# A fused attention and maxout kernel: sums of exponentials tested on chip, with a branch to a recomputing part

## The chip, the cores and the metric

The kernel runs on one core of one Trainium2 chip. The metric is the device time of one launch in microseconds (us); where several runs are shown, their median. The core has five engines with their own instruction streams: TensorE (PE in the profile; PEld are its weight loads), VectorE (DVE), ScalarE (ACT), GpSimd (POOL) and SyncE (SP). SP and POOL issue the DMA transfers here. Engines wait for one another through semaphores.

## The reference

`x` has shape (8, 8, 512, 64) and `state` (8, 8, 32, 64): batch B, head H, rows, depth D. Attention runs in both directions, then a feed-forward part takes the maximum of three products:

```python
scores = scale * np.matmul(x, state.transpose(0, 1, 3, 2))
scores = scores - scores.max(-1, keepdims=True)
a = np.exp(scores)
a /= a.sum(-1, keepdims=True) + 1e-09
xread = np.matmul(a, state)
scores2 = scale * np.matmul(state, x.transpose(0, 1, 3, 2))
# the same softmax over scores2 gives a2
sread = np.matmul(a2, x)
attn = np.concatenate([xread, sread], axis=2)
# heads side by side: 8 * 544 tokens of 512 values
h = np.maximum(np.maximum(x @ w1, x @ w2), x @ w3)
out = h @ w_out
```

The weights `w1`, `w2`, `w3` are 512 x 768 and `w_out` is 768 x 512. The output is 4352 x 512 in float32. The entries of `x` and `state` are normal draws times 0.1.

## The kernel before, in words

The kernel does not subtract the maximum. It takes exp(scale * score) directly (`scores`, L176), sums over the 32 states (`softmax`, L183, tile `den`), and divides. For the other direction (`sread`, L207) it uses the same exponentials as weights, with a block of ones behind `x` that gives the sum over the 512 rows in the same product; its reciprocal is `rd` (L221).

The attention read and the first feed-forward product are joined: `g_cols` forms G = state times the three weight matrices (tile `G`), and `x_maxout` (L270) multiplies G by the transposed attention weights `aT`, which gives the three products for 512 tokens and 128 of the 768 hidden columns at once. Each call of `maxout` (L253) has three accumulators in PSUM (`pw0`, `pw1`, `pw2`). ACT copies the first to SBUF (L264), DVE takes the maximum with the second (L267) and then with the third (L268), into `ht`. `s_maxout` does the same for the 256 state tokens of all batches. `ffn_out` multiplies `ht` by `w_out` (L285), ACT copies the result to `osb` (L292), and a DMA writes it out (L301, L296). The last piece is shared: ACT copies one half (L289) and DVE the other (L290).

PSUM tiles with the tag `pw` rotate through four buffers; the three accumulators of `maxout`, the output accumulator `po` and several transposes all take from these four.

The order of work on each engine is the order in which the Python code records it (the schedule is manual); each engine takes its instructions strictly in that order. The main loop (L382 on) goes over batches 2 to 7. In each it calls `x_maxout(b, m)` for m = 0 to 5, and after each m the functions that were put in `slots[m]`. For the last batch, b = 7, the slots hold `s_maxout(m)` and, for m = 1, 2, 4 and 5, `ffn_out` of the batch before. So around m = 1 of the last batch, PE's queue holds: six matmuls of `x_maxout(7, 1)`, twelve of `s_maxout(1)`, six of `ffn_out(6, 0)`, then six of `x_maxout(7, 2)`. After the loop come six calls of `ffn_out`, and then the end of the program: SP waits for the semaphores of all engines and DMA queues one after another, and two barriers over all engines follow.

Of the kernel before, what the change touches and what calls it, by code (L numbers as in the profile page):

```python
# [8 lines left out]
F32 = mybir.dt.float32  # L9
BF16 = mybir.dt.bfloat16  # L10
AX = mybir.AxisListType
AF = mybir.ActivationFunctionType


@with_exitstack
def kernel(
# [14 lines left out]
    nc = tc.nc  # L31

    B, H, S, D = x.shape
    _, _, Ns, _ = state.shape
# [7 lines left out]
    J = 4  # L42
    HS = H // 2
    NM = d_ff // 128
    XW = H * J * D
    scale = 1.0 / (D ** 0.5)

    const = ctx.enter_context(tc.tile_pool(name="const", bufs=1))
    data = ctx.enter_context(tc.tile_pool(name="data", bufs=1))
    wpool = ctx.enter_context(tc.tile_pool(name="weights", bufs=1))  # L50
    work = ctx.enter_context(tc.tile_pool(name="work", bufs=2))
    pp = ctx.enter_context(tc.tile_pool(name="pp", bufs=2, space=bass.MemoryType.PSUM))
# [15 lines left out]
    def load_x(b):  # L68
        nc.gpsimd.dma_start(  # L69
            out=x_sb[b][:, 0:XW].rearrange("p (h jd) -> p h jd", h=H),  # L70
            in_=x[b].rearrange("h (p j) d -> p h (j d)", j=J))
# [9 lines left out]
    ident = const.tile([128, 128], BF16, name="ident")  # L81
# [27 lines left out]
    warm = const.tile([128, 1], F32, name="warm")  # L109
    nc.scalar.activation(out=warm, in_=zero[:, 0:1], func=AF.Exp, scale=1.0)  # L110
    ats = data.tile([128, B, HS, Ns], BF16, name="ats")

    def keep_busy(n):
        p = pp.tile([128, 1024], F32, tag="two", name="idle")
        for _ in range(n):
            nc.tensor.matmul(p[:, 0:512], zero[:, 0:128], zero, start=True, stop=True)
# [21 lines left out]
    xT, e, a, aT, G, ht, osb = {}, {}, {}, {}, {}, {}, {}  # L138

    def new(d, b, shape, name, bufs=2):  # L140
        d[b] = work.tile(shape, BF16, tag=name, bufs=bufs, name=name)

    def x_transpose(b, g, copy):

        if g == 0:
            new(xT, b, [128, H, 2, 128], "xT")
        p = pp.tile([128, HS, 2, 128], BF16, tag="pw", bufs=4, name="pxt")
        for s in range(HS):
            for jj in range(2):
                nc.tensor.transpose(  # L150
                    p[:, s, jj, :],
                    xv[b][:, 2 * s + g, 2 * jj:2 * jj + 2, :].rearrange("p j d -> p (j d)"), ident)
        copy(out=xT[b].rearrange("p (s g) j t -> p g s j t", g=2)[:, g], in_=p)  # L153

    def x_transpose_dma(b):
        new(xT, b, [128, H, 2, 128], "xT")
        nc.sync.dma_start_transpose(out=xT[b].rearrange("p h j t -> p (h j) t"), in_=x_sb[b][:, 0:XW])

    def scores(b, g0, g1):
# [7 lines left out]
        for jj in range(2):  # L167
            for g in range(g0, g1):
                for s in range(HS):
# [5 lines left out]
                        stop=(g == g1 - 1 and s == HS - 1), skip_group_check=True)  # L175
        nc.scalar.activation(out=e[b][:, :, g0:g1], in_=p, func=AF.Exp, scale=scale)  # L176

    def softmax(b, g0, g1, mul):
        n = g1 - g0
        if g0 == 0:  # L180
            new(a, b, [128, J, 2, HS, Ns], "a")
        den = work.tile([128, J, n, HS], F32, tag=f"den{n}", name="den")
        nc.vector.reduce_sum(out=den, in_=e[b][:, :, g0:g1], axis=AX.X)  # L183
        rden = work.tile([128, J, n, HS], F32, tag=f"rden{n}", name="rden")
        nc.vector.reciprocal(out=rden, in_=den)  # L185
        mul(  # L186
            out=a[b][:, :, g0:g1].rearrange("p j g s n -> p j (g s) n"),
            in0=e[b][:, :, g0:g1].rearrange("p j g s n -> p j (g s) n"),
            in1=rden.rearrange("p j g s -> p j (g s)").unsqueeze(3).to_broadcast((128, J, n * HS, Ns)))
# [14 lines left out]

    late = []

    def sread(b):  # L207

        p = pp.tile([128, 2, 2, D], F32, tag="pw", bufs=4, name="psr")
        for j in range(J):  # L210
            for g in range(2):
                for s in range(HS):
                    xj = xv[b][:, 2 * s + g, j, :]
                    both = bass.AP(xj.tensor, xj.offset,
                                   (xj.ap[0], (XW - ((2 * s + g) * J + j) * D, 2), (1, D)))
                    nc.tensor.matmul(  # L216
                        p[32 * s:32 * s + 32, g], e[b][:, j, g, s, :], both,
                        start=(j == 0 and g == 0), stop=(j == J - 1), skip_group_check=True,
                        tile_position=(0, 32 * s))
        rd = work.tile([128, 2, 1], F32, tag="rd", name="rd")  # L220
        nc.vector.reciprocal(out=rd, in_=p[:, :, 1, 0:1])  # L221
        sr = work.tile([128, 2, D], BF16, tag="sr", bufs=B, name="sr")
        nc.vector.tensor_mul(out=sr, in0=p[:, :, 0, :], in1=rd.to_broadcast((128, 2, D)))
        late.append(lambda: nc.sync.dma_start_transpose(
            out=ats[:, b].rearrange("p s n -> p (s n)"), in_=sr.rearrange("p g d -> p (g d)")))
# [54 lines left out]
    def ffn_out(b, j, split=False):  # L280
        if j == 0:
            osb[b] = work.tile([128, J, d_model], F32, tag="osb", name="osb")
        p = pp.tile([128, d_model], F32, tag="pw", bufs=4, name="po")
        for m in range(NM):
            nc.tensor.matmul(p, ht[b][:, m, j * 128:(j + 1) * 128], wout_sb[:, m, :],  # L285
                             start=(m == 0), stop=(m == NM - 1))
        o = osb[b]
        if split:
            nc.scalar.copy(out=o[:, j, 0:256], in_=p[:, 0:256])  # L289
            nc.vector.tensor_copy(out=o[:, j, 256:512], in_=p[:, 256:512])  # L290
        else:
            nc.scalar.copy(out=o[:, j, :], in_=p)  # L292
        if b == "s":
            for k in range(4 * j, 4 * j + 4):
                r0 = k * SP + S
                (nc.sync if k % 4 < 2 else nc.gpsimd).dma_start(  # L296
                    out=out[r0:r0 + Ns, :], in_=o[32 * (k % 4):32 * (k % 4) + 32, j, :])
            return
        j0 = j if b == B - 1 and j >= 2 else j - 1
        if j == 1 or j == 3 or j0 == j:  # L300
            (nc.sync if b == B - 1 else nc.gpsimd).dma_start(  # L301
                out=out[b * SP:b * SP + S, :].rearrange("(p j) f -> p j f", j=J)[:, j0:j + 1, :],
                in_=o[:, j0:j + 1, :])


    def late_transposes():
        while late:
            late.pop(0)()

    dve, act, pool = nc.vector.tensor_copy, nc.scalar.copy, nc.gpsimd.tensor_copy  # L310
# [3 lines left out]
    states(0, act)  # L314
    for k in range(1, B // 2):
        nc.vector.memset(bds[k], 0.0)
    keep_busy(4)
    dve(out=x0_sb[0], in_=x0_f)
    x_transpose(0, 0, dve)
# [62 lines left out]
    for b in range(2, B):  # L382
        n = b + 1
        slots = [[] for _ in range(NM)]
        if n < B:
            if n == 3:
                slots[0].append(lambda: x_transpose(n, 0, act))
                slots[0].append(lambda: x_transpose(n, 1, dve))
                slots[3].append(lambda: x_transpose_dma(n + 1))
            elif n + 1 < B:  # L390
                slots[0].append(lambda: x_transpose_dma(n + 1))
            at = 1 if n == 3 else 0
            slots[at].append(lambda: scores(n, 0, 2))
            slots[at].append(lambda: softmax(n, 0, 2, nc.gpsimd.tensor_mul))
            slots[2 if n == 3 else 1].append(lambda: g_cols(n, (0, 1)))
            slots[2].append(lambda: a_transpose_dma(n))
            slots[3].append(lambda: sread(n))
            slots[4].append(lambda: g_cols(n, (2, 3)))
            slots[5].append(lambda: g_cols(n, (4, 5)))
            slots[4].append(late_transposes)  # L400
            if n % 2 and n + 1 < B:
                slots[3].append(lambda: states((n + 1) // 2, act))
            for k in ((4, 5) if n == 3 else (n + 2,)):
                if k < B:
                    slots[0].append(lambda k=k: load_x(k))
        else:
            for m in range(NM):
                slots[m].append(lambda m=m: s_maxout(m))
        for m in (1, 2, 3, 4, 5) if len(pending) > 4 else (1, 2, 4, 5):
            if pending:  # L410
                slots[m].append(lambda t=pending.pop(0): ffn_out(*t))
        for m in range(NM):
            x_maxout(b, m)
            for f in slots[m]:
                f()
        pending += [(b, j) for j in range(J)]
# [4 lines left out]
    ffn_out("s", 1)  # L421
    ffn_out(B - 1, 2)
    ffn_out(B - 1, 3, split=True)


# [28 lines left out]
```

## Time and profile before

| what | value |
|---|---|
| time, median of 3 runs | 166.25 us (166.08 to 167.53) |
| span of the profiled execution, first to last instruction | 164.5 us |
| left between that span and the median | about 1.8 us |
| PE busy | 149.7 us, 91% of the span |
| DVE busy | 96.0 us, 58% |
| ACT busy | 99.1 us, 60% |
| POOL busy | 44.0 us, 27% |

The profiled execution has no time of its own apart from its span; the median minus the span is what the launch adds around it. Busy PE includes the modelled ends of matmuls that overlap, so it is not a share of the peak. An engine's busy time leaves out register, branch, semaphore and DMA-issuing instructions.

### The profile page before, as it was taken

To read this page: it belongs to the slowest core of one execution; us is meant where nothing else is said; L and a number is where in the kernel's file an instruction comes from. 1 tells how busy PE (TensorE), PEld (TensorE's weight loads), DVE (VectorE), ACT (ScalarE), POOL (GpSimd) and SP (SyncE) were. 2 spreads that over 40 slices of the span, in tenths; PEclk is the share of its full clock that TensorE was granted. 3 is DMA by queue.
4 is the path that set the end of the run, shared out by engine and by line. 5 is a ranking of instruction groups with operands and counts; after the bars stand their busy time and mean duration, and the time that the engine had idled before them with its cause. 6 is when DMAs were issued, how large, how long until landed. Compare 5 with 4: busy or idle time off the path is not lost.

```text
span 164.5 us, 3569 instructions
## 1 busy us (share of the span) xinstructions
PE 149.7 (91%) x1432; PEld 70.9 (43%) x1449; DVE 96.0 (58%) x162; ACT 99.1 (60%) x158; POOL 44.0 (27%) x64
## 2 busy tenths in 40 slices
PE   7658699988999999999999999999999999999990
PEld 2425243533445444434344434444444466665430
DVE  4675777889418553665548464865586455585001
ACT  3355578366896678853876688648755853333440
POOL 8975550106150601081016101410141010100140
PEclk9999999999999999999999999999999999999999
DMA  4999999800039999269992989460306030030373
GB/s 132 195 174 199 204 200 248 122 7 0 0 120 130 144 256 198 53 116 145 277 193 87 133 187 104 162 191 14 128 0 195 8 130 0 0 132 0 128 235 148
DMA packets 31824, 20.94 MB, mean 127 GB/s; under 512 B 17184, under 2 KB 29344, under 8 KB 31808
## 3 DMA queue, kind: packets, MB, share of 16 engines
q0 software_dynamic: 15632, 15.08, 46.3%
q1 hardware_dynamic: 16176, 5.64, 18.5%
q8 instruction: 11, 0.18, 0.5%
q14 instruction: 5, 0.04, 0.1%
HBM read 15.20 MB, written 8.91 MB: 147 GB/s over the span
## 4 chain that ended last, share of the span: by engine, by line
PE 63%; DVE 11%; ACT 10%; DMA 6%; POOL 4%; issue 4%; DVEq 0%; ACTq 0%; POOLq 0%
PE pw L260 34%; PE po L285 20%; DMA x<-in_x_dram 4%; PE pg L239 4%; DVE den L183 4%; DVE t L267 3%; ACT e L176 3%; ACT G L245 3%; DVE ht L268 3%; PE ps L171 2%; ACT t L264 2%; PE psr L216 2%; POOL w L94 1%; DMA out_dram<-osb 1%; POOL a L186 1%
## 5 line engine op out<-in xcount | busy, mean ns | idle before, releaser
L260 PE MATMUL pw<-aT,G 128*128 128x512 bf16 x288 | 71.2, 379 | 3.6 <-ACT G L245 1.8
L267 DVE TENSOR_TENSOR t<-t,pw 128x512 bf16<-128x512 bf16 (+1 forms) x54 | 35.1, 650 | 41.6 <-ACT t L264 40.0
L285 PE MATMUL po<-wout,ht 128*128 128x512 bf16 x188 | 47.9, 380 | 0.8
L260 PEld LDWEIGHTS <-G 128*128 128x128 bf16 x288 | 26.7, 98 | 36.2 <-issue 5.1
L245 ACT CAST G<-pg 128x768 bf16<-128x768 f32 x48 | 36.5, 805 | 8.0 <-PE pg L239 7.6
L264 ACT CAST t<-pw 128x512 bf16<-128x512 f32 (+1 forms) x54 | 30.5, 566 | 14.1 <-PE pw L260 12.6
L268 DVE TENSOR_TENSOR ht<-t,pw 128x512 bf16<-128x512 bf16 (+1 forms) x54 | 35.5, 658 | 5.6
L292 ACT COPY osb<-po 128x512 f32<-128x512 f32 x33 | 19.4, 587 | 21.2 <-PE po L285 20.7
L285 PEld LDWEIGHTS <-ht 128*128 128x128 bf16 x204 | 18.4, 98 | 23.6 <-issue 4.7
L301 POOL DMA_DIRECT2D out_dram<-osb x14 | 7.8, 559 | 70.2 <-ACT osb L292 70.2
L186 POOL TENSOR_TENSOR a<-e,rden 128x1024 bf16<-128x1024 bf16 (+1 forms) x8 | 14.4, 1800 | 33.4 <-DVE rden L185 19.8
L239 PE MATMUL pg<-w,bd 64*32 64x384 bf16 x384 | 13.0, 328 | 1.1 <-DMA w<-in_moe_w_dram 1.1
L183 DVE TENSOR_REDUCE den<-e 128x32 f32<-128x1024 bf16 (+1 forms) x9 | 9.9, 1095 | 2.6 <-ACT e L176 2.6
L176 ACT ACTIVATE e<-ps 128x1024 bf16<-128x1024 f32 x7 | 7.2, 1024 | 5.8 <-PE ps L171 5.8
L260 PE MATMUL pw<-ats,w 128*128 128x256 bf16 x72 | 8.8, 273 | 0.0
L239 PEld LDWEIGHTS <-bd 64*32 64x32 bf16 x384 | 3.6, 89 | 11.7 <-issue 11.7
L260 PEld LDWEIGHTS <-w 128*128 128x128 bf16 x72 | 7.0, 98 | 2.1
L94 POOL DMA_DIRECT2D w<-in_moe_w_dram x9 | 6.8, 770 | 0.0
L69 POOL DMA_DIRECT2D x<-in_x_dram x7 | 6.7, 957 | 0.0
L150 PE MATMUL pxt<-ident,x 128*128 128x128 bf16 x64 | 4.4, 219 | 2.2 <-DMA x<-in_x_dram 1.1
L134 ACT COPY bd<-pt 64x512 bf16<-64x512 bf16 x6 | 3.5, 580 | 4.2 <-PE pt L131 4.1
L171 PEld LDWEIGHTS <-xT 128*128 128x128 bf16 x128 | 4.7, 98 | 2.4 <-DVE xT L153 0.8
(42 smaller groups left out, 63.4 us busy)
## 6 DMA issues: line engine op xcount, KB each, us to landing
out_dram<-osb POOLq DMA_DIRECT2D x14, 512.0 KB, 3.7
x<-in_x_dram POOLq DMA_DIRECT2D x7, 512.0 KB, 9.0
w<-in_moe_w_dram POOLq DMA_DIRECT2D x3, 384.0 KB, 10.3
w<-in_moe_w_dram POOLq DMA_DIRECT2D x3, 256.0 KB, 8.2
wout<-in_moe_w_out_dram POOLq DMA_DIRECT2D x1, 768.0 KB, 16.4
x0f<-in_x_dram SPq DMA_DIRECT2D x1, 512.0 KB, 4.0
out_dram<-osb SPq DMA_DIRECT2D x1, 512.0 KB, 2.7
out_dram<-osb SPq DMA_DIRECT2D x2, 256.0 KB, 2.2
```

The source lines that it names most:

```text
L94: nc.gpsimd.dma_start(out=w_sb[c][:, :, i, :], in_=w.rearrange("(kk p) f -> p kk f", p=128)[:, :, m0 * 128:m1 * 128])
L176: nc.scalar.activation(out=e[b][:, :, g0:g1], in_=p, func=AF.Exp, scale=scale)
L183: nc.vector.reduce_sum(out=den, in_=e[b][:, :, g0:g1], axis=AX.X)
L186: mul(out=a[b][:, :, g0:g1].rearrange("p j g s n -> p j (g s) n"), in0=e[b][:, :, g0:g1].rearrange("p j g s n -> p j (g s) n"), in1=rden.r ...
L239: nc.tensor.matmul(p[32 * s:32 * s + 32, g, 0:384].rearrange("p (i f) -> p i f", i=3), bd(b, 2 * s + g)[64 * g:64 * g + 64, g, :], w[64 * ...
L245: copy(out=G[b][:, :, m * 384:(m + 1) * 384], in_=p[:, :, 0:384])
L260: nc.tensor.matmul(p[:, 0:n], lhs(i, k), rhs(k), start=(k == 0), stop=(k == nk - 1))
L264: nc.scalar.copy(out=t0[:, 0:n], in_=pw[0][:, 0:n])
L267: nc.vector.tensor_max(t1[:, 0:n], t0[:, 0:n], pw[1][:, 0:n])
L268: nc.vector.tensor_max(ht[b][:, m, :], t1[:, 0:n], pw[2][:, 0:n])
L285: nc.tensor.matmul(p, ht[b][:, m, j * 128:(j + 1) * 128], wout_sb[:, m, :], start=(m == 0), stop=(m == NM - 1))
L292: nc.scalar.copy(out=o[:, j, :], in_=p)
```

## The change

Four things are done. First, the sums of exponentials (`den`) and the reciprocals of the other direction (`rd`) are no longer put in rotating tiles but kept, for all batches, in one tile `seen` of 128 x 8 x 34. Second, a function `check_range` takes the maximum and the minimum of `seen` on DVE, compares them with 1e18 and 1e-18, adds up the 256 answers over partitions with one matmul against a tile of ones (PE), and writes an integer `flag`. It is put in `slots[1]` of the last batch, ahead of `s_maxout(1)`. Third, a memset of `ones` on POOL is added near the start. Fourth, at the end all five engines load `flag` into a register (`values_load`) and branch on it: if it is not zero, a part follows that recomputes all batches with the maximum subtracted.

```diff
+    seen = data.tile([128, B, J * H + 2], F32, name="seen")
...
-        den = work.tile([128, J, n, HS], F32, tag=f"den{n}", name="den")
+        den = seen[:, b, 0:J * H].rearrange("p (j g s) -> p j g s", j=J, g=2)[:, :, g0:g1]
...
-        rd = work.tile([128, 2, 1], F32, tag="rd", name="rd")
+        rd = seen[:, b, J * H:J * H + 2].unsqueeze(2)
...
+    flag = data.tile([128, 1], I32, name="flag")
+    ones = const.tile([128, 128], BF16, name="ones")
+
+    def check_range():
+        v = seen.rearrange("p b k -> p (b k)")
+        top = work.tile([128, 2], F32, tag="top", name="top")
+        nc.vector.tensor_reduce(out=top[:, 0:1], in_=v, op=ALU.max, axis=AX.X)
+        nc.vector.tensor_reduce(out=top[:, 1:2], in_=v, op=ALU.min, axis=AX.X)
+        ok = work.tile([128, 2], BF16, tag="ok", name="ok")
+        nc.vector.tensor_scalar(out=ok[:, 0:1], in0=top[:, 0:1], scalar1=1e18, scalar2=None, op0=ALU.is_le)
+        nc.vector.tensor_scalar(out=ok[:, 1:2], in0=top[:, 1:2], scalar1=1e-18, scalar2=None, op0=ALU.is_ge)
+        p = pp.tile([128, 2], F32, tag="pw", bufs=4, name="pst")
+        nc.tensor.matmul(p, ones, ok, start=True, stop=True)
+        n = work.tile([128, 1], F32, tag="nok", name="nok")
+        nc.vector.reduce_sum(out=n, in_=p, axis=AX.X)
+        nc.vector.tensor_scalar(out=flag, in0=n, scalar1=255.5, scalar2=None, op0=ALU.is_le)
...
+    nc.gpsimd.memset(ones, 1.0)
     keep_busy(4)
...
         else:
+            slots[1].append(check_range)
             for m in range(NM):
                 slots[m].append(lambda m=m: s_maxout(m))
...
+    bad = nc.values_load(flag[0:1, 0:1], min_val=0, max_val=1)
+    with tc.If(bad != 0):
+        for b in range(B):
+            x_transpose(b, 0, act)
+            x_transpose(b, 1, dve)
+            scores_below_max(b)
+            softmax(b, 0, 2, nc.vector.tensor_mul)
+            a_transpose(b, 0, act)
+            a_transpose(b, 1, dve)
+            sread_below_max(b)
+            late_transposes()
+            for m in range(NM):
+                g_cols(b, (m,))
+            for m in range(NM):
+                x_maxout(b, m)
+            for j in range(J):
+                ffn_out(b, j)
+        for m in range(NM):
+            s_maxout(m)
+        ffn_out("s", 0)
+        ffn_out("s", 1)
```

In the program as built, the recomputing part stands between the kernel's main part and its end. It has 3437 instructions on PE, 317 on DVE, 272 on ACT, 35 on POOL and 29 on SP, and each engine jumps over its own when the flag is zero. Where it is jumped over, a short part takes its place, in which each engine raises its semaphores by what the recomputing part would have added: one instruction each on PE, DVE and ACT, eight on SP, five on POOL. SP's series of closing waits grows from nine instructions to twelve, and each engine's load of the flag waits only for DVE's last step of `check_range`.

More of the change, by code (lines that the diff above doesn't have):

```diff
@@ L12 @@
 AF = mybir.ActivationFunctionType
+ALU = mybir.AluOpType
+I32 = mybir.dt.int32
 @with_exitstack
@@ L205, with sread @@
     late = []
-    def sread(b):
+    def sread(b, e=e):
         p = pp.tile([128, 2, 2, D], F32, tag="pw", bufs=4, name="psr")
@@ L423, with scores_below_max @@
     ffn_out(B - 1, 3, split=True)
+    def scores_below_max(b):
+        new(e, b, [128, J, 2, HS, Ns], "e")
+        p = pp.tile([128, J, 2, HS, Ns], F32, tag="two", name="ps")
+        for jj in range(2):
+            for h in range(H):
+                nc.tensor.matmul(
+                    p[:, 2 * jj:2 * jj + 2, h % 2, h // 2, :], xT[b][:, h, jj, :],
+                    bd(b, h).rearrange("p c n -> p (c n)"),
+                    start=(h == 0), stop=(h == H - 1), skip_group_check=True)
+        mx = work.tile([128, J, 2, HS], F32, tag="mx", bufs=1, name="mx")
+        nc.vector.tensor_reduce(out=mx, in_=p, op=ALU.max, axis=AX.X)
+        sc = work.tile([128, J * H, Ns], F32, tag="sc", bufs=1, name="sc")
+        nc.vector.tensor_sub(
+            out=sc, in0=p.rearrange("p j g s n -> p (j g s) n"),
+            in1=mx.rearrange("p j g s -> p (j g s)").unsqueeze(2).to_broadcast((128, J * H, Ns)))
+        nc.scalar.activation(out=e[b].rearrange("p j g s n -> p (j g s) n"), in_=sc, func=AF.Exp, scale=scale)
@@ new lines, in sread_below_max @@
+    def sread_below_max(b):
+        p = pp.tile([128, 2, 2, 2, 128], F32, tag="two", name="ps")
+        for h in range(H):
+            s, g = h // 2, h % 2
+            for c in range(2):
+                nc.tensor.matmul(
+                    p[32 * s:32 * s + 32, c, g], bd(b, h)[64 * c:64 * c + 64, c, :],
+                    xT[b][64 * c:64 * c + 64, h, :, :],
+                    start=(g == 0), stop=(g == 1), tile_position=(64 * c, 32 * s), skip_group_check=True)
+        mx = work.tile([128, 2], F32, tag="mx2", bufs=1, name="mx2")
+        nc.vector.tensor_reduce(out=mx, in_=p.rearrange("q c g i t -> q g c (i t)"), op=ALU.max, axis=AX.XY)
+        nc.vector.tensor_scalar(out=mx, in0=mx, scalar1=-scale, scalar2=None, op0=ALU.mult)
+        eT = work.tile([128, 2, 2, 2, 128], BF16, tag="eT", bufs=1, name="eT")
+        for g in range(2):
+            nc.scalar.activation(
+                out=eT[:, g].rearrange("q c i t -> q c (i t)"),
+                in_=p[:, :, g].rearrange("q c i t -> q c (i t)"),
+                func=AF.Exp, scale=scale, bias=mx[:, g:g + 1])
+        new(e, b, [128, J, 2, HS, Ns], "e")
+        for g in range(2):
+            p = pp.tile([128, 2, 2, 128], BF16, tag="pw", bufs=4, name="pat")
+            for c in range(2):
+                for i in range(2):
+                    nc.tensor.transpose(p[:, i, c, :], eT[:, g, c, i, :], ident)
+            nc.scalar.copy(out=e[b][:, :, g].rearrange("p j s n -> p j (s n)"),
+                           in_=p.rearrange("p i c k -> p (i c) k"))
+        sread(b)
```

## The prediction

> **What bounds the kernel now.** I read the page first, then the stretch where the check is put and the end, by windows and by timeline. The page's first two parts:
>
> ```profile
> PE 149.7 (91%) x1432; PEld 70.9 (43%) x1449; DVE 96.0 (58%) x162; ACT 99.1 (60%) x158; POOL 44.0 (27%) x64
> ...
> PE   7658699988999999999999999999999999999990
> ...
> PEclk9999999999999999999999999999999999999999
> ```
>
> PE is the bound from about the tenth slice to the last but one, at full granted clock. What matters is whether it has any slack where the check lands. The busy time by stretch (span, then each engine's busy us):
>
> ```profile
> 135.40:138.20 2.80, 2.75 (x19) 1.86 (x19) 2.10 (x4) 0.37 (x1) 0.00 (x0) 1.00 0.00 0
> 138.20:150.00 11.80, 11.75 (x74) 7.20 (x74) 6.66 (x13) 4.93 (x10) 0.53 (x1) 1.00 0.12 46
> 150.00:160.20 10.20, 10.15 (x52) 4.94 (x51) 1.86 (x4) 3.89 (x7) 2.54 (x5) 1.00 0.42 142
> 135.40:160.20 24.80, 24.64 (x142) 14.00 (x143) 10.61 (x20) 9.19 (x18) 3.08 (x6) 1.00 0.23 80
> ```
>
> PE is busy 24.64 of the last 24.80 us. One round of the last batch (six matmuls of 512 columns for x, twelve of 256 for the states, six for the output) takes 3.90 us, from 135.41 to 139.31 in the timeline: 216 ns for each 512 columns, with no hole. So a hole made here moves the end by its whole length. The place itself, where m = 1 of the last batch runs:
>
> ```profile
> 134.12 1.46 PE L260 MATMUL pw<-aT,G 128*128 128x512 bf16 x6
> 134.75 0.59 ACT L264 CAST t<-pw 128x512 bf16<-128x512 f32 x1 [0.93 <-PE pw L260]
> 135.37 0.69 DVE L267 TENSOR_TENSOR t<-t,pw 128x512 bf16<-128x512 bf16 x1 [0.21 <-ACT t L264]
> 135.41 1.47 PE L260 MATMUL pw<-ats,w 128*128 128x256 bf16 x12
> 136.16 0.69 DVE L268 TENSOR_TENSOR ht<-t,pw 128x512 bf16<-128x512 bf16 x1
> ```
>
> PE goes on to the state tokens at 135.41, while DVE is still at the maxima of the x tokens until 136.85. The check is recorded between the two. And the end:
>
> ```profile
> 159.61 1.89 SPq L301 DMA_DIRECT2D out_dram<-osb  x2
> 160.29 0.37 ACT L289 COPY osb<-po 128x256 f32<-128x256 f32 x1 [0.71 <-PE po L285]
> 160.70 0.42 DVE L290 COPY osb<-po 128x256 f32<-128x256 f32 x1 [8.63 <-DMA out_dram<-osb]
> ```
>
> ```profile
> SPq L449 <- DMA out_dram<-osb: 1.6, 2, 1.2
> ```
>
> After DVE's copy (to 161.12) SP issues the last DMA, which lands at 163.17; SP waited 1.2 us for it. In the trace's records SP then works through its closing waits at one per 61 ns (163.19 to 163.56), drains at 163.62, and two barriers end the span at 164.46: 0.84 us.
>
> **Part by part.** *Sums kept in `seen`*: the same 9 reductions, 9 + 8 reciprocals and 8 multiplications, of the same shapes, in the same places and with the same waits. Nothing, either way. *Memset of `ones`*: one instruction on POOL. A 128x128 memset took 205 ns (the one of `ident`). POOL's next work is the first attention multiply, for which it waited 0.9 us on DVE, and that wait hides it; uncovered it would be 0.2 us.
>
> *The check on DVE.* Two reductions of 128x272 float32. Rows: 128x512 took 658 ns and 128x1024 took 1220 ns, a line of 96 ns + 1.10 ns per element, so 0.39 us each. Those rows read bf16; if this type or operation differs, the ends are 0.27 (the memset of 128x256) and 0.66 (the 512 row whole). I take 0.40. Two comparisons of 128x1: nearest is the reciprocal of 128x2, 157 ns; ends 0.10 (memsets of 128x1) and 0.29 (the 128x128 multiply of L223). After ht at 136.85: maximum to 137.27, minimum to 137.68, and with 0.04 us between dependent DVE steps (reciprocal to multiply, 126.11 to 126.15) the comparisons end at 138.04.
>
> *The matmul of the check on PE* is the expensive place. It needs those answers, and behind it in PE's queue stand the twelve matmuls of the states, `ffn_out(6, 0)` and everything after; for them wait ACT and DVE. A PE instruction starts about 0.06 us after DVE's end (5.89 to 5.95, the first transposes), so it runs at 138.10; the next weight load stands behind it and leads its matmul by some 0.1 to 0.2 us (135.20 to 135.41). The states start at 138.26 instead of 135.41: **2.85 us**, almost none of it work. Ends, with the row bounds above: 2.3 and 3.5. The accumulators of the states find free `pw` buffers by then. The last two DVE steps (sum of two, comparison; 0.16 us each) run while PE fills the first state accumulator and hold nobody; uncovered, 0.4 us.
>
> *The branch at the end.* It adds, on each engine, a load of the flag, a compare and a jump; the profile of before shows none of them. Times here are those of before; all shift by 2.85.
> SP alone: 1.2 us of waiting for the last landing covers its load and check if these are short. From 163.19 it has six raises of DMA semaphores, one jump and twelve waits, where before there were six waits: 13 more steps at 61 ns, **0.8 us**. That is the floor of this term.
> Then the others: the end of SP's series needs the raises that DVE, PE and ACT make behind their jumps, and DVE starts last: its sequencer was past the last copy's dispatch at 160.71. For its load I bound by one semaphore step, 0.06, and by a small DMA's issue to landing, 2.1 us (the four 64 KB writes of SP), and take the nearest thing that loads an engine's inner state, ACT's table load, 1.28 us. For the jump: the page has PE's instructions arriving in pieces on a queue of their own,
>
> ```profile
> q8 instruction: 11, 0.18, 0.5%
> q14 instruction: 5, 0.04, 0.1%
> ```
>
> 0.18 MB in 11 packets (16 KB each, for PE) and 0.04 MB in 5 (8 KB each, 128 instructions of 64 bytes; the other engines), spread over the span, so code is not all on hand. DVE's target lies 317 instructions ahead, over two such pieces. The cost is between nothing (it is there) and 4.0 us (issue to landing of 128 KB of weights); I take the slower small row, 2.3 us (POOL's 64 KB writes), and 0.5 for the piece's packet, 2.8. DVE raises its semaphore at 160.71 + 1.28 + 2.8 + two steps = 164.91; SP has three waits left and drains at 165.13, not 163.62: **+1.5 us**, which includes the 0.8.
>
> [...]
>
> **Sum.** 2.85 + 1.5 = 4.35 us on a span of 164.46, so 168.8, and with the 1.8 us around it 170.6; equally 166.25 + 4.35, since the median is that span and what lies around it.
>
> **Rivals.**
> *A. The jumps cost more, or SP's own misses.* If SP's code is not on hand either, SP is at 161.55 + 1.28 + 2.8 + 0.2 = 165.8, and only then works through eight raises and twelve waits, 1.2 us: drain at 167.0, a term of 3.4: 172.5. Against it: only 29 instructions are jumped. The same time comes if load and fetch on DVE reach their upper ends (166.9).
> *B. The clock falls in the hole.* The longest PE idle with the clock kept is 1.1 us (at 11.6); a hole of 2.7 is not shown. If the granted clock went to half for as long as the 3.4 us it took from first matmul to full clock here (warm at 4.2), 1.7 us would be lost: 172.3. [...]
> *C. Not slower: the hole is paid back.* While PE stands, ACT and DVE empty the four `pw` buffers; if PE lost time later to those buffers, it would now run through, and the landing would cover the jumps. It decides if PE's later idle reaches the hole's 2.85 us. The windows show 0.16. Time: 166.3 to 167, even if all was right with it.
> *D. The check is short and the jumps are on hand:* 2.3 + 0.8, or 169.3; a load of almost nothing leaves 169 to 169.9.
> *E. The flag comes out nonzero* and all is recomputed: another 150 us or more (PE's busy time again). Scores of entries of 0.1 give sums near 32 and reciprocals near 1/512, far inside the bounds.
>
> **Chances.** Forecast, 170.0 to 171.6: 0.45. D, 168.4 to 170.0: 0.22. A, 171.6 to 173.4: 0.22. B: 0.05. C: 0.04. E and the rest: 0.02. The range from 168.8 to 173.0 holds the forecast, most of D, A and B. A measurement of this kernel can tell about 1%, 1.7 us, from no change. All cases but C are slower by more, so slower 0.95, same 0.03, faster 0.02.
>
> **What would show it.** In the changed profile, a hole on PE ahead of the check's matmul of 2.5 to 2.8 us, released by DVE; the check's reductions at 0.4 us; PE full again behind it, clock at 1.00; PE's last matmul some 2.85 us later; from the last landing to the span's end some 2.8 us instead of 1.3. The prediction fails if the hole is under 2 us, if anything after it takes time back, or if the end takes under 1.5 us or over 5.

## The result, and the profile after

The changed kernel takes 171.97 us (median of 5 runs, 171.27 to 174.24), the kernel before 166.91 us in the 5 runs beside which it stands now (166.08 to 167.58). The ratio is 1.0307, with a 95% interval from 1.0251 to 1.0363: slower by about 5.1 us. The prediction was 170.6, with a range from 168.8 to 173.0.

The profiled execution is the slowest of the five (174.24 us, span 172.5); the granted clock fell to one half twice in it, from 9.86 to 13.28 us and from 139.57 to 142.98, behind the check, and the comparison leaves that run out. It is read below by stretches, so that what belongs to the clock can be told from the rest.

The first two parts of the page of the changed kernel (busy time; busy tenths and clock in 40 slices):

```profile
PE 153.1 (89%) x1433; PEld 72.4 (42%) x1450; DVE 97.3 (56%) x168; ACT 99.1 (57%) x158; POOL 44.1 (26%) x65
...
PE   7867799889999999999999999999999589999920
...
PEclk9969999999999999999999999999999969999997
```

One slice of PE has dropped to 5 and the clock is at 6 tenths in the slice behind it; at the end there are two slices with little or nothing of PE, not one. These are the three places where time went. The first of them in the timeline (start, length, engine, line, what, idle before and releaser):

```profile
136.75 0.69 DVE L271 TENSOR_TENSOR ht<-t,pw 128x512 bf16<-128x512 bf16 x1
137.36 0.43 DVE L318 TENSOR_REDUCE top<-seen 128x1 f32<-128x272 f32 x1
137.70 0.42 DVE L319 TENSOR_REDUCE top<-seen 128x1 f32<-128x272 f32 x1
138.04 0.14 DVE L321 TENSOR_SCALAR ok<-top 128x1 bf16<-128x1 f32 x1
138.16 0.16 DVE L322 TENSOR_SCALAR ok<-top 128x1 bf16<-128x1 f32 x1
138.37 0.16 PE L324 MATMUL pst<-ok,ones 128*128 128x2 bf16 x1 [2.20 <-DVE ok L322]
...
138.40 1.63 PE L263 MATMUL pw<-ats,w 128*128 128x256 bf16 x12
```

PE stands for 2.20 us until DVE's comparisons are done, and the state tokens of m = 1 follow at once. What comes behind, by windows (span; busy us of PE, PEld, DVE, ACT, POOL; granted clock; DMA):

```profile
135.00:140.00 5.00, 2.80 (x20) 1.81 (x19) 3.63 (x11) 0.96 (x2) 0.00 (x0) 0.96 0.11 46
140.00:145.00 5.00, 4.78 (x22) 2.37 (x21) 1.39 (x3) 1.54 (x3) 0.00 (x0) 0.70 0.00 0
145.00:150.00 5.00, 5.00 (x33) 2.99 (x31) 3.07 (x7) 1.62 (x4) 0.53 (x1) 1.00 0.25 102
```

The clock record has it at one half from 139.57 to 142.98. And the end, in the timeline and in the DMA issues of the stretch from 158 us on (count, size, median us from issue to landing; the instruction queues above them):

```profile
161.73 3.67 SPq L299 DMA_DIRECT2D out_dram<-osb  x4
...
164.96 0.37 ACT L292 COPY osb<-po 128x256 f32<-128x256 f32 x1 [0.71 <-PE po L288]
165.36 0.42 DVE L293 COPY osb<-po 128x256 f32<-128x256 f32 x1 [8.63 <-ACT osb L292]
165.49 0.87 SPq L304 DMA_DIRECT2D out_dram<-osb  x2
```

```profile
q8 instruction: 2, 0.03, 1.5%
q14 instruction: 5, 0.04, 0.9%
...
out_dram<-osb SPq DMA_DIRECT2D x2, 256.0 KB, 4.3
```

The same two writes in the kernel before:

```profile
out_dram<-osb SPq DMA_DIRECT2D x2, 256.0 KB, 2.2
```

From the start of DVE's last copy to the end it now takes 7.09 us, before 3.76. Two pieces of PE's code (16 KB each) and five of the other engines' (8 KB) are fetched from 158 us on, and the two last writes land 4.3 us after their issue where it was 2.2.

The operations of the changed kernel at the branch (engine, operation; ns min/median/max; first and last start), and SP's two waits there (us in total, times, longest):

```profile
L496 SPq EVENT_SEMAPHORE  x8: 17/17/17, 169.7 to 170.8; - x8
...
L496 PEldq COMPARE_BRANCH  x1: 4117/4117/4117, 161.7 to 161.7; - x1
...
L496 DVEq COMPARE_BRANCH  x1: 72/72/72, 166.0 to 166.0; - x1
...
L496 SPq COMPARE_BRANCH  x1: 45/45/45, 167.4 to 167.4; - x1
...
L496 DVEq EVENT_SEMAPHORE  x1: 21/21/21, 169.9 to 169.9; - x1
```

```profile
SPq L496 <- SPq L496: 2.8, 2, 2.2
```

The profile names SP itself as the one that released it, because each of these steps both waits for the semaphore of a write and raises it. The landing times tell more: the last write but one landed at 169.69 us and SP's first step ran at 169.70, the last write landed at 170.30 and SP's second step ran at 170.31. So SP waited for two late writes; these waits are not the length of its jump.

The best reading of every run of this case is by four numbers of its profiled execution: from the start of the state tokens of m = 0 to those of m = 1 (the hole lies there); from there to the start of DVE's last copy (a fall of the clock would lie there); from that copy to the span's end (the tail); and, inside the tail, from the issue of the last write to the landing of its last part. The last columns are the ratio to the kernel before over the timed runs, and its interval.

| kernel | hole stretch | to last copy | tail | landing | ratio | interval |
|---|---|---|---|---|---|---|
| before | 2.60 | 25.28 | 3.76 | 2.02 | | |
| after | 5.00 | 26.97 | 7.09 | 4.34 | 1.0307 | 1.0251 to 1.0363 |
| e1 sums kept alone | 2.60 | 25.29 | 3.76 | 2.02 | 1.0020 | 0.9957 to 1.0083 |
| e2 check alone | 5.00 | 26.85 | 3.76 | 2.02 | 1.0182 | 1.0077 to 1.0286 |
| e3 branch alone | 2.61 | 25.29 | 6.72 | 3.98 | 1.0146 | 1.0072 to 1.0220 |
| e4 branch over one memset | 2.60 | 25.29 | 3.79 | 2.01 | 0.9989 | 0.9939 to 1.0038 |
| e5 branch over one batch | 2.60 | 25.28 | 5.94 | 4.17 | 1.0120 | 1.0067 to 1.0172 |
| e6 check, hole filled | 5.00 | 25.28 | 3.77 | 2.03 | 1.0128 | 1.0089 to 1.0167 |
| e7 check split | 2.61 | 25.60 | 3.77 | 2.03 | 1.0028 | 0.9987 to 1.0068 |
| e8 branch far for PE alone | 2.60 | 25.28 | 6.17 | 4.40 | 1.0135 | 1.0052 to 1.0217 |
| e9 branch far for DVE and ACT alone | 2.61 | 25.28 | 5.23 | 2.56 | 1.0117 | 1.0074 to 1.0159 |
| e10 after, check split | 2.60 | 25.59 | 6.55 | 3.72 | 1.0215 | 1.0168 to 1.0263 |
| e11 after, again | 5.00 | 26.84 | 6.48 | 3.65 | 1.0292 | 1.0242 to 1.0342 |
| e12 after, hole filled | 5.00 | 25.28 | 6.68 | 4.07 | 1.0350 | 1.0281 to 1.0419 |

### The profile page after: what moved, and what is told of

Its sections match the earlier page's. It is cut to its first block, busy times and chain, and to the rows that moved or that the text cites. A ratio compares the mean times of both kernels' runs of the same rounds, so it can differ in the third digit from the quotient of the medians.

```text
span 172.5 us, 3609 instructions
## 1 busy us (share of the span) xinstructions
PE 153.1 (89%) x1433; PEld 72.4 (42%) x1450; DVE 97.3 (56%) x168; ACT 99.1 (57%) x158; POOL 44.1 (26%) x65
## 4 chain that ended last, share of the span: by engine, by line
PE 63%; DVE 11%; ACT 10%; DMA 5%; issue 4%; POOL 4%; DVEq 0%; ACTq 0%; POOLq 0%
PE pw L263 32%; PE po L288 22%; DMA x<-in_x_dram 5%; PE pg L242 4%; DVE seen L186 4%; DVE t L270 3%; DVE ht L271 3%; ACT e L179 3%; ACT G L248 3%; ACT t L267 2%; PE ps L174 2%; PE psr L219 2%; POOL w L96 1%; POOL a L189 1%; ACT osb L295 1%
## 5 line engine op out<-in xcount | busy, mean ns | idle before, releaser
L288 PE MATMUL po<-wout,ht 128*128 128x512 bf16 x188 | 49.1, 387 | 1.0 <-issue 0.2
L271 DVE TENSOR_TENSOR ht<-t,pw 128x512 bf16<-128x512 bf16 (+1 forms) x54 | 35.5, 658 | 5.6
L186 DVE TENSOR_REDUCE seen<-e 128x32 f32<-128x1024 bf16 (+1 forms) x9 | 9.9, 1095 | 2.6 <-ACT e L179 2.6
L119 PE MATMUL idle<-zero 128*128 128x512 bf16 x12 | 5.9, 630 | 1.4 <-DVE zero L82 1.2
```

Of the source, the lines that this page charges most:

```text
L271: nc.vector.tensor_max(ht[b][:, m, :], t1[:, 0:n], pw[2][:, 0:n])
```

## The experiments

After the result the theory was: the hole at the check costs 2.4 us, a fall of the clock behind it up to 1.7 us in part of the executions, and the tail 2.5 to 3.3 us, because the engines jump to code that is not on hand. The rivals are in the expectations.

### The four parts of the change, one at a time

**Sums kept alone (e1).**

```diff
-    nc.gpsimd.memset(ones, 1.0)
...
-            slots[1].append(check_range)
...
-    bad = nc.values_load(flag[0:1, 0:1], min_val=0, max_val=1)
-    with tc.If(bad != 0):
...
```

> Only the sums are kept in one tile; no check, no branch. Theory (the cost is a hole at the check's matmul of about 2.4 us, a clock that falls in it in part of the runs, and a tail of about 3 us from jumps to code that is not on hand): no difference, 0.0 us, ratio 1.000. Rival (one tile shared by all batches adds waits or slower writes on DVE): 0.3 us or more, with longer reductions or new waits on DVE before the check's place.

Measured: 166.63 us against 167.01, ratio 1.002 with an interval that holds 1, and all four stretches as before to 0.01 us. The rival falls: keeping the sums in one tile costs nothing.

**Check alone (e2).**

```diff
-    bad = nc.values_load(flag[0:1, 0:1], min_val=0, max_val=1)
-    with tc.If(bad != 0):
...
```

> The check without load and branch; the recomputing part is left out and the flag is read by nobody. Theory: PE stands 2.2 us ahead of the check's matmul and the time grows by 2.4 us where the granted clock stays, by up to 4.1 us where it falls to half for 3.4 us behind the hole. Rival (the hole alone, the fall of the clock being a chance of one profile): 2.4 us in all runs and a mean granted clock of 1.00. Rival (the tail holds nearly all of it): under 1 us.

Measured: ratio 1.018, 3.0 us with an interval from 1.3 to 4.8 us. The hole stretch grows by 2.40 us and the tail is untouched, so the rival that the tail holds nearly all falls. The stretch behind grows by 1.57 us in the profiled execution: the clock record has one half from 138.39 to 141.80. But the one timed run at a mean clock of 1.00 took 168.31 us, 1.3 us over the median before; so the fall is in part of the runs only.

**Branch alone (e3).**

```diff
-    nc.gpsimd.memset(ones, 1.0)
+    nc.vector.memset(flag, 0)
...
-            slots[1].append(check_range)
```

> No check: the flag is set to zero at the start, then load, branch and the recomputing part as in the changed kernel. The range is not tested. Theory: 2.5 to 3.3 us, all of it behind the last copy; DVE and ACT take 3.5 to 3.9 us from their compare to the next instruction. Rival (load of the flag and the longer series of semaphore steps on SP alone): 1.5 us at most.

Measured: ratio 1.015 (2.4 us), tail 6.72, so 2.96 us longer. The rival with 1.5 us at most falls. DVE's compare is at 160.74 and its next instruction at 164.58, ACT's at 160.40 and 163.65: stalls of 3.8 and 3.2 us, as the theory has it. But they do not end last. SP's first step behind its jump waits for the last write but one (landed at 163.15, the step at 163.17), its second for the last write (164.65 and 164.66). DVE raised its semaphore at 164.58, when SP still had some 1 us of steps ahead of its wait for it. The landing, 3.98 us after the issue instead of 2.02, set the end.

**Branch over one memset (e4).**

```diff
     with tc.If(bad != 0):
-        for b in range(B):
...
+        nc.vector.memset(warm, 0.0)
```

> As the run with the branch alone, but the part that is jumped over holds one memset on DVE and nothing else, so every target is at most a few instructions ahead. Nothing is recomputed and the range is not tested. Theory (missing code): jumps of 0.1 to 0.3 us, SP is back before the last write lands, and 0.3 us is left for four more semaphore steps. Rival (load and compare are what costs): 1.3 us or more. Rival (the last write lands late for another reason): its landing stays 3 to 4 us after its issue here too.

Measured: ratio 0.999, tail 3.79. Load, compare and jump are all there. Two views of this kernel, its operations at the branch (engine, operation; ns min/median/max; first and last start) and its DMA issues from 155 us on:

```profile
L495 PEldq COMPARE_BRANCH  x1: 220/220/220, 156.7 to 156.7; - x1
...
L495 ACTq COMPARE_BRANCH  x1: 45/45/45, 160.8 to 160.8; - x1
L495 DVEq COMPARE_BRANCH  x1: 72/72/72, 161.0 to 161.0; - x1
...
L495 SPq COMPARE_BRANCH  x1: 53/53/53, 162.1 to 162.1; - x1
```

```profile
out_dram<-osb SPq DMA_DIRECT2D x2, 256.0 KB, 2.1
```

PE's compare is over in 0.22 us, and in the trace's records the next instruction on ACT, DVE and SP starts 0.17 to 0.23 us after the compare. The write lands 2.0 us after its issue. Both rivals fall. A branch as such costs this kernel nothing: everything it does fits in the 2 us in which the last write is under way.

### What in the branch costs

**Branch over one batch (e5).**

```diff
-        for b in range(B):
+        for b in range(1):
...
-        for m in range(NM):
-            s_maxout(m)
-        ffn_out("s", 0)
-        ffn_out("s", 1)
```

> As the run with the branch alone, but the part that is jumped over recomputes one batch only: 409 instructions on PE, 40 on DVE, 37 on ACT, 5 on POOL, 3 on SP. The range is not tested. Theory (a jump costs by whether the target's piece of code of 128 instructions, 256 on PE, is on hand): DVE, ACT and SP jump in 0.1 to 0.3 us unless a border of a piece lies between, PE stalls some 4 us but starts early enough; 0.3 to 1.0 us in all. Rival (any jump forward stalls alike, whatever the distance): 2.5 to 3.3 us, as with the whole part.

The piece sizes named there, and the 64 bytes of the prediction, fit the trace of the kernel before: between the starts of the second and the eleventh of its 16 KB pieces (25.83 and 145.68 us) it has 1120 matmuls and 1133 weight loads, 250 instructions of PE for each piece, or 65 bytes for each instruction. The 8 KB pieces that start at 51.80 and 132.74 lie 127 of ACT's records apart, those at 35.62 and 111.44 132 of DVE's; that these pieces are theirs is an estimate from the counts.

Measured: ratio 1.012 (2.0 us), tail 5.94, 2.18 us longer. This is where my theory was incomplete. ACT, DVE, SP and POOL all go on 0.17 to 0.58 us after their compare, as expected; PE stalls 4.1 us but is back at 161.43, early. By the theory that should leave 0.3 to 1.0 us. The rival is wrong too, since the distance does decide the stalls. What SP waits for is in its waits:

```profile
SPq L536 <- DMA out_dram<-osb: 2.3, 1, 2.3
```

The last write, issued at 161.25, has 14 of its 16 parts landed at 163.29, one at 163.50 and the last at 165.42. The packet records show the second piece of PE's code, 16 KB, starting at 162.17 and taking 1.81 us. So the next theory: PE's code pieces arrive on the DMA engines that also move the last write, and hold up the part that comes behind them.

**Far for PE alone (e8).**

```diff
     with tc.If(bad != 0):
-        for b in range(B):
...
+        nc.vector.memset(warm, 0.0)
+        keep_busy(600)
```

> As the run with the branch alone, but the part that is jumped over holds 600 dummy matmuls with their weight loads on PE (1201 instructions) and one memset on DVE; the other engines jump over two instructions at most. Nothing is recomputed, the range is not tested. Theory (the pieces of PE's code, 16 KB each, come on the same DMA engines as the last write and hold one part of it up): PE stalls 4 us, the others 0.2 us, SP is back before the last write would land, yet that write lands 3.5 to 4.5 us after its issue instead of 2.0; 1.5 to 2.5 us in all. Rival (only stalls of DVE, ACT and SP behind their jumps count, and the late landing with one recomputed batch was chance): landing 2.0 us after issue, 0.0 to 0.5 us in all.

Measured: ratio 1.014 (2.2 us, interval 0.9 to 3.6), tail 6.17. Its operations at the branch, SP's waits, and the issues from 155 us on:

```profile
L495 PEldq COMPARE_BRANCH  x1: 3717/3717/3717, 159.3 to 159.3; - x1
...
L495 DVEq COMPARE_BRANCH  x1: 72/72/72, 163.5 to 163.5; - x1
```

```profile
SPq L523 <- DMA out_dram<-osb: 2.7, 2, 2.1
```

```profile
q8 instruction: 2, 0.03, 1.0%
...
out_dram<-osb SPq DMA_DIRECT2D x2, 256.0 KB, 4.5
```

PE alone is held, for 3.7 us, and goes on at 163.07, before the last write is even issued (163.34). Nothing on the other engines stalls, SP is back at 164.79, and yet the write lands at 167.74 instead of some 165.35, when 15 of its parts are there. The rival falls: 2.4 us of tail come from fetching PE's code, without any stall that anyone waits for. That the late part sits behind the 16 KB piece (163.76, for 1.92 us) on one DMA engine is what times and sizes say; the records name no engine, so that step is argued and not shown.

**Far for DVE and ACT alone (e9).**

```diff
     with tc.If(bad != 0):
-        for b in range(B):
...
+        for _ in range(300):
+            nc.vector.memset(warm, 0.0)
+            nc.scalar.copy(out=sp1, in_=zero[:, 0:1])
```

> The reverse: the part that is jumped over holds 300 memsets on DVE and 300 copies on ACT and nothing on PE, POOL and SP. Nothing is recomputed, the range is not tested. Theory: DVE and ACT stall 3.3 to 3.9 us behind their jumps, no 16 KB piece is fetched, the last write lands at most 2.8 us after its issue; SP then waits for DVE's raise some 4.4 us after the last copy began, which gives 0.9 to 1.5 us in all. Rival (pieces of 8 KB hold the write up just as well): landing 3.5 us or more after its issue. Rival (stalls of DVE and ACT are covered by the landing): under 0.5 us.

Measured: ratio 1.012 (1.9 us, interval 1.2 to 2.6), tail 5.23, 1.47 us longer. SP's waits and the issues:

```profile
SPq L525 <- DVEq L496: 0.9, 1, 0.9
SPq L525 <- DMA out_dram<-osb: 0.8, 1, 0.8
```

```profile
q14 instruction: 4, 0.03, 0.5%
...
out_dram<-osb SPq DMA_DIRECT2D x2, 256.0 KB, 2.4
```

Here SP does wait for DVE's raise: compare at 160.96, next instruction at 164.37, 3.4 us. The write lands 2.56 us after its issue, two parts of it 0.5 us late. Both rivals fall: pieces of 8 KB hold the write up little, and the stalls are not covered once the landing is early. So two things lie beside each other in the tail, 1.5 us from stalls on DVE and 2.2 to 2.4 us from the late landing; in the changed kernel the longer covers the shorter.

### What in the check costs

**Hole filled (e6).**

```diff
-    bad = nc.values_load(flag[0:1, 0:1], min_val=0, max_val=1)
-    with tc.If(bad != 0):
...
+            slots[1].append(lambda: keep_busy(10))
             slots[1].append(check_range)
```

> The check without load and branch, with ten matmuls of zeros (512 columns, 2.2 us) put into PE's queue ahead of the check's matmul, where PE otherwise stands. Nothing is recomputed. Theory (the hole lasts as long as DVE takes, and what comes on top of it is the clock): the same hole as far as the end is concerned, 2.4 to 2.5 us, but no fall of the clock in any run, so the spread of the check alone is gone. Rival (PE idle is no cause of the fall): clock falls here as often as with the check alone. If the clock never falls in the check alone either, both come out equal at 2.4 us.

Measured: ratio 1.013 (2.1 us; runs from 168.00 to 168.54). Windows of the check alone (first line) and of this kernel (second), where the same work runs 1.4 us earlier:

```profile
136.00:141.00 5.00, 2.80 (x15) 1.83 (x14) 2.99 (x9) 0.46 (x2) 0.00 (x0) 0.74 0.00 0
```

```profile
136.00:141.00 5.00, 4.95 (x31) 2.76 (x29) 2.25 (x9) 1.39 (x3) 0.00 (x0) 1.00 0.00 0
```

The hole stretch is 5.00 in both, so DVE's answers set it and not PE; the clock is 0.74 in the one and 1.00 in the other, and the stretch behind is 26.85 and 25.28. The rival (idleness is no cause) finds no support, in one profiled execution each.

**Check split (e7).**

```diff
...
+        oks.append(ok)
+
+    oks = []
+
+    def check_sum():
+        ok = oks.pop()
         p = pp.tile([128, 2], F32, tag="pw", bufs=4, name="pst")
...
             slots[1].append(check_range)
+            slots[2].append(check_sum)
...
-    bad = nc.values_load(flag[0:1, 0:1], min_val=0, max_val=1)
-    with tc.If(bad != 0):
...
```

> The check without load and branch, split: the four DVE steps stay where they are, the matmul and the two steps behind it are recorded one round later (behind the x tokens of m = 2). Nothing is recomputed. Theory (the hole is PE waiting for DVE's answers): no hole, clock 1.00, and 0.0 to 0.4 us for DVE's 0.8 us of new work, which PE's four accumulators cover. Rival (it is the work itself, or the weight change on PE, that costs): 2 us or more again.

Measured: ratio 1.003 with an interval that holds 1; the hole is gone and 0.31 us are added behind it. The matmul itself in the timeline of this kernel:

```profile
139.90 0.17 PE L330 MATMUL pst<-ok,ones 128*128 128x2 bf16 x1
...
139.91 0.69 DVE L270 TENSOR_TENSOR t<-t,pw 128x512 bf16<-128x512 bf16 x1 [0.73 <-ACT t L267]
139.93 1.76 PE L263 MATMUL pw<-ats,w 128*128 128x256 bf16 x12
...
140.66 0.75 PEld L263 LDWEIGHTS <-w 128*128 128x128 bf16 x7 [0.30 <-issue]
```

The matmul and the weight change take 0.03 us of PE. The rival falls: it was the wait, not the work. The 0.31 us that stay are in the state tokens behind it (1.76 us instead of 1.47): the weight loads stand for 0.30 us until 140.66, and DVE's step at 139.91 ends at 140.60. The check's result takes one of the four `pw` buffers, so the second accumulator of the states has to wait for the buffer which that step frees; this follows from the order and the times, and no run tests it.

### Parts together

**The whole change with the check split (e10).** The split of e7 on the changed kernel, with load and branch kept.

> The whole changed kernel with the check split as before: its matmul and the two steps behind it one round later. Nothing is left out. Theory (hole and tail add up and have nothing to do with each other): the tail of the branch alone, 2.2 to 2.7 us, and 0.3 us for the split check; 2.5 to 3.0 us over the kernel before, some 2.3 us or more under the changed kernel. Rival (the branch costs more once the check is in): 4 us or more.

Measured: 169.20 us against 165.87, ratio 1.0215 (3.6 us, interval 2.8 to 4.4). In the stretches 0.31 and 2.79 us, 3.1 in sum: a little over what was expected. The ratio alone, whose interval holds both 3.0 and 4.0, does not decide between theory and rival; the stretches speak for the sum of the two parts, since neither grew. Nothing is left out of this kernel, and its ratio lies under the changed kernel's 1.0307 and 1.0292, with intervals that overlap by 0.001 and 0.002. It is the best version that tests the range; the kernel before, which does not, is faster.

**The changed kernel again (e11), and with the hole filled (e12).** The second has the added line of e6.

> The changed kernel once more, beside the next one on one chip. Theory (hole 2.4 us, tail 2.7 to 3.3 us, and up to 1.7 us where the clock falls behind the hole): 5.1 to 7.4 us over the kernel before, differing from run to run by the clock. Rival (the clock does not matter): 5.1 to 5.7 us in all runs.

> The changed kernel with ten matmuls of zeros in PE's queue ahead of the check's matmul; nothing is left out. Theory (idle PE is what makes the clock fall): hole and tail stay, the fall goes; 5.1 to 5.7 us over the kernel before in all runs, as much under the changed kernel as the clock had cost there, 0.5 to 1.7 us. Rival (the fall comes without regard to the hole, or costs nothing): both kernels alike.

Measured: 171.16 and 171.78 us against 165.98, ratios 1.029 and 1.035, intervals that overlap. In the profiled executions the stretch behind the hole is 26.84 in the first and 25.28 in the second: the fall of the clock (one half from 138.93 to 142.34) is there in the one and not in the other, 1.56 us. In the timed runs filling the hole gained nothing. Six runs of the changed kernel, from 170.56 to 171.58 us, have a mean clock of 0.994 or 0.996; 3.4 us at half clock are 0.010 of the span, so they can hold no such fall. The rival of e11 (5.1 to 5.7 us without regard to the clock) holds for its median of 5.2; two of its six runs, 174.24 and 175.61 us, lie above both ranges. So the profiled executions speak for the hole as the cause of the fall (there in three of three with the hole open, in none of two with it filled), but the fall does not come in all executions, and the ratios owe little or nothing to it. How often it comes was not measured.

## Why the prediction came out as it did

- *Sums kept in one tile, memset of ones:* costed at nothing; e1 shows 0.00 in every stretch.
- *The hole:* 2.85 us forecast, 2.40 measured in every execution that has the check as written. Mechanism and place were right: PE idle 2.20 us, released by DVE's comparisons. Mis-sized was the chain of DVE. The four steps took 0.43, 0.42, 0.14 and 0.16 us, near the rows taken, but without waits between them they overlap: the reductions start 0.34 us apart, the first of them 0.08 us before the row of L271 ends, the comparisons 0.12 apart. The chain from L271's end to PE's start is 0.93 us, not 1.25. The allowance for the weight load, 0.16, was 0.03. The ends given for the hole, 2.3 and 3.5, leave that 0.16 out; with it the same rows give 2.5 and 3.6, so 2.40 lies inside them only by that slip.
- *No slack behind the hole:* right. In e6 the stretch behind it is 25.28 as before; nothing is paid back (rival C), and nothing more is lost when the clock stays.
- *The flag load:* 1.28 us taken for DVE, measured 0.54 there and 0.50 to 0.73 elsewhere. *The jump:* 2.8 taken, measured 3.86 on DVE (165.995 to 169.858) and 3.4 to 3.8 in the experiments. The sum of the two, 4.1, against 4.5 measured (165.378 to 169.858), is so near by luck in part: one term was too long, the other too short. The stall behind a jump was 0.2 us over one memset (e4), 3.2 to 3.9 us over some 300 instructions on DVE and ACT (e3 and the changed kernel), and 3.7 to 4.2 us on PE (e5, e8 and the changed kernel). Loading the flag took 0.50 to 0.82 us (the changed kernel and e9).
- *The tail, the step that was wrong:* 1.5 us forecast, 2.7 to 3.3 measured (e3, e11 and after). I let the last landing stay where it was and had DVE's raise end last. In the changed kernel the landing came 2.3 us late, and DVE's raise at 169.88 was there 1.5 us before SP asked for it. The tail's 3.33 us are 2.32 of later landing, 0.83 of SP's longer series behind it (from the landing to SP's drain 1.28 instead of 0.45, close to the 0.8 forecast), 0.14 of a later issue and 0.04 in the barriers. That DVE's stall costs 1.5 us where nothing covers it is what e9 shows (1.47); it is only not what ends last here. By an estimate from these steps, with both writes on time and SP back before DVE, SP's drain would follow DVE's raise by 0.19 us, at some 170.1 instead of 171.6, and 1.8 us of longer tail would be left.
- *SP's own misses (rival A):* not shown. SP's first step behind its jump comes 2.26 us after its compare in the changed kernel (1.0 to 2.3 in e3, e10, e11 and e12, 0.2 where the part was small), but in all five kernels it runs 0.02 us after the landing of the last write but one, which it waits for; in the changed kernel that write landed 4.20 us after its issue. The jump itself took at most 1.0 us in e3, and how long it takes alone stays open. The changed kernel came near rival A's 172.5, but by late writes.
- *The clock (rival B):* given 0.05, and there in the profiled execution, where it cost 1.69 us behind the hole (26.97 instead of 25.28). That execution was also 0.59 us late when the state tokens of m = 0 began, with another half clock from 9.86 to 13.28 before. The median owes little to it. That a hole of this length would keep the clock, as so low a chance has it, no run showed: the longest idle time of PE in the kernel before was 1.1 us. In the changed kernel PE stood for 2.20 us until 138.37, and the clock was at one half for 3.41 us from 139.57. The prediction's 3.4 us from the first matmul to full clock are 3.0 in the trace (1.19 to 4.20).
- *The signs it named:* the hole of 2.20 us is under the 2.5 to 2.8 named, and from the last landing to the end it took 2.16 us instead of 2.8, since the landing itself came late. Neither crossed the bounds at which it was to fail.
- *Total:* 4.35 forecast, 5.1 measured; too little in the tail by 1.2 to 1.8, too much in the hole by 0.45. That the two errors took part of each other away is luck.

## What to carry to other kernels

The check's matmul, which waited 2.20 us for DVE's answers, held up all that was queued behind it on PE; recorded one round later, the same check cost 0.3 us instead of 2.4. A branch at the end cost nothing where what it jumps over was small on every engine, PE included (e4: ratio 0.999, tail 3.79 us against 3.76). Where it was large, not only the stalls behind the jumps counted (1.47 us of tail in e9) but also the landing of the last output write, 2.6 to 4.4 us after its issue instead of 2.0, since SP's last steps waited for it. And when the tail is to be judged, measure it from the last copy to the end: without a far jump that stretch repeated to 0.03 us (3.76 to 3.79) in kernels whose total times differed by 2 us from run to run. With one it does not: 7.09 and 6.48 us in two executions of the same kernel.

## What was not expected of the hardware

- Output writes landed late while code was fetched: with a far jump on PE alone (e8), one of 16 parts of a 256 KB write landed 2.4 us after the others, with one 16 KB piece of code fetched between its issue and its landing.
- One of SP's issues was long as well: while the first 16 KB piece of the tail came in the changed kernel (162.75, for 1.68 us), one issue of a 64 KB write by SP took 1.81 us, where the two before it took 0.35 and 0.41; in e9, which fetches no 16 KB piece, all four took 0.31 to 0.41.
- The clock fell to one half for 3.4 us after 2.2 us of idleness on PE, in the three profiled executions with the open hole (e2, e11 and after) and in neither of the two with the hole filled.
